# Moving GpSimd's range test of the softmax sums ahead of its last two stores

## The chip, the cores and the metric

The kernel runs on one core of one Trainium2 chip. A core has a matrix engine (TensorE, PE in the profile; PEld is its weight load), a vector engine (VectorE, DVE), a scalar engine (ScalarE, ACT), a general engine (GpSimd, POOL) and a queue engine that only issues transfers (SyncE, SP). Each engine runs its own list of instructions in order, and the lists meet through semaphores. Data moves between memory and the core's buffers by DMA. The metric is the time of one execution on the device, in microseconds (us).

## The reference

Sort-net attention, followed by a token mixer. Batch 4, 8 heads, 768 tokens, 64 values per head, 8 blocks of 96 tokens, model width 512.

```python
P = sort_net                                   # (B, H, 8, 8)
for _ in range(5):
    P = exp(P - max(P, -1))
    P = P / (sum(P, -1) + 1e-09)
    P = P / (sum(P, -2) + 1e-09)
k_sorted, v_sorted = P @ k_blocks, P @ v_blocks
scores = scale * q_b @ k_sorted.T              # per block of 96
attn = exp(scores - max(scores))
attn = attn / (sum(attn, -1) + 1e-09)
x = attn @ v_sorted                            # (B, S, 512) over all heads
W_tok = moe_scale * (x @ w_q) @ (x @ w_k).T    # per batch
out = relu(W_tok @ x) @ w_out
```

## The kernel before

**Order.** Everything is laid out by hand. The string ORDER (lines 18 to 50) lists some 450 steps, and a loop at the end of the kernel (lines 670 to 680) issues them one by one. A step's first letter is its kind, the first digit is the batch, and the rest is a part of that batch. Capital letters are TensorE steps with the PSUM bank that they write. Small letters are the steps that read that bank, with an engine (A ScalarE, D VectorE, G GpSimd, S the SyncE queue). So `r34:D:2` is the normalization's reciprocal of batch 3, group 4, on VectorE. The list fixes the order of each engine's own instructions; between engines, only semaphores order the work.

**Stages of a batch.** K and V are sorted by the 8x8 matrices (K, V, and k, v to move them out of PSUM), scores are formed (S), ScalarE takes their exponentials without subtracting a maximum (e), TensorE multiplies by V with a column of ones so that the sum of each row comes out beside the product (P), VectorE takes the reciprocals of the sums into `Rall` (r, line 399) and multiplies by them (x, line 404). After that come transposes (D as DMA, T on TensorE), the projections (J, j, d), the mixer's products (W, w, G, g, H, h), the output projection (O, with o to move it out of PSUM) and the stores (s). Four batches overlap; the last one is batch 3.

**The range test.** Since no maximum is subtracted, a sum could leave the range of the number format. The kernel keeps all reciprocals of all batches in `Rall` (96 partitions by 280 values) and tests them with GpSimd in `guard()` (lines 504 to 516): the largest value (a reduction across the partitions), a multiplication of the whole tile by -1 in place, the largest again, four operations on a single value, and a load of the resulting flag into a GpSimd register. Line 684 branches on that register. If the flag is set, GpSimd computes the whole result again in a slow and safe way (`general`, lines 518 to 667, a very long straight list of instructions); with the given inputs it is not set, and the branch jumps over that list.

**GpSimd's last steps in the kernel before**, in the order of the list: `d21:G` (a copy into `qD`, line 166), `d30:G` (the same for batch 3), the stores `s21:G` and `s20:G` of batch 2 (line 492, 512 KB each), then the range test, then the branch, then what the branch's join waits for (recorded under line 684), then the end of the program (line 713), where all engines drain and meet. The other stores of the end are issued from SP and from ACT (lines 492 and 497).

Of the kernel before, what the change touches and what calls it, by code (L numbers as in the profile page):

```python
# [41 lines left out]
R30:S R34:S S34:4 J20:3 e35:A:6 h10:D:0 J21:2 R33:S j21:D:2 H11:0 e34:A:4 P32:4 j20:A:3 r32:D:4  # L42
h11:A:0 P30:6 P31:2 s01:S x32:D:4 r31:D:2 x31:D:2 d21:G O15:0 P33:4 o15:A:0 r30:D:6 O10:1 P34:2
o10:A:1 O14:0 N20:S o14:A:0 O11:1 G20:0 s00:S x30:D:6 D30:S r34:D:2 G21:0 r33:D:4 o11:A:1 x33:D:4
g20:A:0 x34:D:2 D31:S d20:A O12:6 s02:S H20:4 H21:0 s10:S H22:2 O13:7 h20:A:4 O20:4 h21:A:0 O23:5
h22:D:2 o13:D:7 J31:2 o12:A:6 j31:A:2 J30:0 O22:1 W31:7 j30:A:0 W30:6 w30:D:6 O21:3 o23:D:5 s12:S
w31:A:7 o20:D:4 o21:D:3 G30:0 s11:S d30:G d31:A G31:0 o22:A:1 s21:G g30:D:0 O25:7 s20:G H32:2 H30:4
H31:0 h32:A:2 O24:6 h30:D:4 h31:D:0 o24:A:6 O34:3 O30:5 o34:A:3 O32:2 O31:4 o25:A:7 o30:D:5 o32:A:2
s34:S O33:0 s22:S o31:D:4 s30:S O315:7 s32:A O35:6 s31:S o33:A:0 o315:A:7 o35:A:6 s33:S s35:A
"""  # L50


# [1 line left out]
def kernel(  # L54
# [12 lines left out]
    B, H, S, D = q.shape  # L67
# [43 lines left out]
    names = {x.split(":")[0] for x in ORDER.split()}  # L111
# [116 lines left out]
    def u_l(b, n, e, bank):  # L228
        if n == "p":
            for s, w in enumerate((moe_w_q, moe_w_k)):  # L230
                nc.gpsimd.dma_start(out=w16[:, s * DM // 2:(s + 1) * DM // 2],  # L231
                                    in_=w.rearrange("(p u) d -> p (u d)", p=P))
        elif n == "o":
            nc.gpsimd.dma_start(out=wo, in_=moe_w_out.rearrange("(t p) d -> p t d", p=P))
        else:
            t, src = {"q": (Qn, q), "k": (Kn, k), "v": (Vn, v)}[n[0]]
            h0, h1 = {"": (0, H), "a": (0, H // 2), "b": (H // 2, H)}[n[2:]]
            b = int(n[1])
            nc.gpsimd.dma_start(out=t[b % NIN][:, h0:h1].rearrange("p h r d -> p h (r d)"),  # L239
                                in_=src[b, h0:h1].rearrange("h (p r) d -> p h (r d)", p=P))  # L240
# [263 lines left out]
    def guard():  # L504
        s1 = keep.tile([1, 2], FP32, name="s1")
        flag = keep.tile([1, 1], mybir.dt.int32, name="flag")
        g = nc.gpsimd
        rv = Rall.rearrange("p b n a t -> p (b n a t)")
        g.tensor_reduce(s1[:, 1:2], rv, axis=AX.XYZWC, op=ALU.max)
        g.tensor_scalar(rv, rv, -1.0, None, op0=ALU.mult)  # L510
        g.tensor_reduce(s1[:, 0:1], rv, axis=AX.XYZWC, op=ALU.max)
        g.tensor_scalar(s1[:, 0:1], s1[:, 0:1], -1e-20, None, op0=ALU.is_le)
        g.tensor_scalar(s1[:, 1:2], s1[:, 1:2], 1e20, None, op0=ALU.is_le)
        g.tensor_tensor(s1[:, 0:1], s1[:, 0:1], s1[:, 1:2], op=ALU.mult)
        g.tensor_scalar(flag, s1[:, 0:1], -1.0, 1.0, op0=ALU.mult, op1=ALU.add)
        return g.value_load(flag[0:1, 0:1])
# [153 lines left out]
    for item in ORDER.split():  # L670
        kind, arg = item[0], item.split(":")[1:]
        if kind == "l":
            u_l(0, item[1:].split(":")[0], None, None)
            continue
        name = item.split(":")[0]
        b, n = int(name[1]), int(name[2:])
        if kind.isupper() and kind not in "RND":
            fns[kind](b, n, int(arg[0]))
        else:
            fns[kind](b, n, arg[0], int(arg[1]) if len(arg) > 1 else None)  # L680

    off = guard()
    work.close()
    with tc.If(off > 0):
        with tc.tile_pool(name="gp", bufs=1) as gp, \
# [32 lines left out]
```

## Time and profile before

| | us |
|---|---|
| median of 3 runs | 100.3 (99.89 to 100.78) |
| the profiled execution | 100.55 |
| its span, first to last instruction | 98.6 |
| granted TensorE clock | 0.997 |
| TensorE busy in the span | 87.9 (89%) |
| ScalarE busy | 71.4 (72%) |
| VectorE busy | 67.3 (68%) |
| GpSimd busy | 31.0 (31%) |
| read from HBM, written to it | 20.19 MB, 6.29 MB |

The profiled execution lies inside the range of the runs, and 1.95 us of its time lie outside the span. Times in the profile count from the span's start. A line number is a line of the kernel; line 160 is the helper through which all matmuls go, lines 164, 166 and 168 are the copies of ScalarE, GpSimd and VectorE. A name such as POOLq or SPq is the engine's instruction queue: branches, semaphore waits, register loads and the issue of transfers stand under it and do not count as busy time. Instructions are themselves brought in by DMA; the profile lists those transfers as queues of the kind "instruction".

### The profile page before, as it was taken

The page shows a single profiled execution, that of the slowest core. Times are in us where ns is not written, and L with a number is a line of the kernel's source. Part 1 is how long each engine was busy: PE and PEld are TensorE (multiplying, and loading weights), DVE is VectorE, ACT ScalarE, POOL GpSimd, SP SyncE. Part 2 cuts the span into 40 slices and gives each one's busy share as a digit, 9 for nine tenths or more (in the row PEclk, how much of TensorE's full clock was granted, in tenths as well). Part 3 has the DMA queues.
Part 4 walks back from the last instruction along what each step waited for, and adds up shares of the span by engine and source line. Part 5 has one row for each costly group of instructions (what it writes and reads, how often), then busy time and mean ns, then how long its engine had stood idle before and what let it go on. Part 6 is the DMA issues. An engine that isn't in the chain of part 4 may idle for free.

```text
span 98.6 us, 3365 instructions
## 1 busy us (share of the span) xinstructions
PE 87.9 (89%) x1429; PEld 59.1 (60%) x1429; DVE 67.3 (68%) x130; ACT 71.4 (72%) x104; POOL 31.0 (31%) x55
## 2 busy tenths in 40 slices
PE   4999697898999999899999999999699999999800
PEld 2346466777888678676676768845565445454400
DVE  2677799779999578987731998956599250965200
ACT  5236876899976998998999989799435765466500
POOL 7973859497009790000000200000200002296000
PEclk9999999999999999999999999999999999999998
DMA  0799999999999999999999996699752999394990
GB/s 10 283 373 200 203 205 204 202 207 203 205 232 249 246 200 206 204 204 240 245 237 206 203 188 87 162 168 260 279 214 54 212 367 415 130 352 174 394 360 6
DMA packets 25488, 21.67 MB, mean 220 GB/s; under 512 B 8192, under 2 KB 23552, under 8 KB 25472
## 3 DMA queue, kind: packets, MB, share of 16 engines
q0 software_dynamic: 12544, 10.36, 63.6%
q1 hardware_dynamic: 12496, 10.44, 36.0%
q10 hardware_dynamic: 432, 0.66, 2.0%
q8 instruction: 11, 0.18, 0.7%
q14 instruction: 5, 0.04, 0.1%
HBM read 20.19 MB, written 6.29 MB: 269 GB/s over the span
## 4 chain that ended last, share of the span: by engine, by line
PE 48%; ACT 15%; DMA 15%; DVE 6%; SPq 5%; POOL 4%; issue 2%; POOLq 0%; ACTq 0%; DVEq 0%
PE ps L160 48%; DMA Kn<-in_k_dram 12%; ACT E L375 7%; DVE X L404 4%; ACT Vs L164 4%; ACT KT L164 3%; DMA VT<-Vs 3%; SPq L410 2%; SPq L336 2%; POOL ot L231 1%; ACT ot L164 1%; POOL Vn L239 1%; DVE Rall L399 1%; DVE QT L168 1%; POOL qkT L221 1%
## 5 line engine op out<-in xcount | busy, mean ns | idle before, releaser
L375 ACT ACTIVATE E<-ps 96x960 bf16<-96x960 f32 (+1 forms) x28 | 23.5, 906 | 1.6 <-PE ps L160 1.4
L160 PE MATMUL ps<-wo,mixT 128*128 128x512 bf16 (+1 forms) x100 | 23.3, 371 | 0.0
L404 DVE TENSOR_TENSOR X<-ps,Rall 96x896 bf16<-96x896 f32 (+1 forms) x20 | 20.0, 1006 | 0.7
L160 PEld LDWEIGHTS <-mixT 128*128 128x128 bf16 x125 | 11.5, 102 | 13.4 <-issue 4.0
L166 POOL COPY qD<-qkT 64x384 bf16<-64x384 bf16 x4 | 2.0, 502 | 45.6 <-ACT qkT L164 31.1
L164 ACT COPY ot<-ps 128x512 f32<-128x512 f32 (+2 forms) x20 | 11.2, 569 | 6.2 <-PE ps L160 6.1
L164 ACT CAST KT<-ps 128x768 bf16<-128x768 f32 x13 | 10.1, 807 | 2.9 <-PE ps L160 2.8
L160 PE MATMUL ps<-VT,E 96*128 96x65 bf16 x256 | 11.0, 193 | 0.9 <-DMA VT<-Vs 0.8
L160 PEld LDWEIGHTS <-E 96*128 96x128 bf16 x256 | 9.5, 97 | 3.2 <-issue 1.0
L260 POOL TENSOR_TENSOR M<-PTR,m_p 128x512 bf16<-128x512 bf16 x6 | 7.8, 1315 | 8.4 <-PE ps L160 7.2
L160 PEld LDWEIGHTS <-KT 64*128 64x128 bf16 (+1 forms) x288 | 8.2, 97 | 3.2 <-issue 2.1
L160 PE MATMUL ps<-QT,KT 64*128 64x96 bf16 x256 | 8.8, 204 | 0.3 <-ACT KT L164 0.3
L467 ACT ACTIVATE mixT<-ps 128x1024 bf16<-128x1024 f32 x7 | 7.1, 1026 | 2.4 <-PE ps L160 2.3
L469 DVE TENSOR_SCALAR mixT<-ps 128x1024 bf16<-128x1024 f32 x5 | 6.0, 1223 | 3.8 <-PE ps L160 3.6
L160 PE MATMUL ps<-M,Kn 128*64 128x128 bf16 x192 | 7.4, 221 | 0.6 <-DMA Kn<-in_k_dram 0.5
L160 PE MATMUL ps<-mixT 128*128 128x512 bf16 x25 | 7.9, 482 | 0.0
L168 DVE CAST KT<-ps 128x768 bf16<-128x768 f32 x7 | 6.5, 953 | 1.1 <-PE ps L160 1.1
L399 DVE RECIPROCAL Rall<-ps 96x14 f32<-96x14 f32 (+1 forms) x20 | 4.4, 226 | 4.0 <-PE ps L160 3.7
L164 ACT COPY QT<-ps 128x768 bf16<-128x768 bf16 x9 | 6.8, 807 | 0.5 <-PE ps L160 0.4
L160 PE MATMUL ps<-idb,Qn 128*64 128x128 bf16 x192 | 6.7, 220 | 0.2 <-POOL Qn L166 0.2
L160 PEld LDWEIGHTS <-Kn 128*64 128x64 bf16 x192 | 5.8, 109 | 1.6 <-DMA Kn<-in_k_dram 0.7
L160 PEld LDWEIGHTS <-Qn 128*64 128x64 bf16 x192 | 5.7, 110 | 0.9 <-issue 0.4
(88 smaller groups left out, 125.3 us busy)
## 6 DMA issues: line engine op xcount, KB each, us to landing
out_dram<-ot SPq DMA_DIRECT2D x7, 512.0 KB, 3.7
Vn<-in_v_dram POOLq DMA_DIRECT2D x4, 768.0 KB, 13.8
Kn<-in_k_dram POOLq DMA_DIRECT2D x4, 768.0 KB, 13.9
Qn<-in_q_dram POOLq DMA_DIRECT2D x3, 768.0 KB, 16.3
VT<-Vs SPq DMA_DIRECT2D x17, 132.0 KB, 6.4
XT<-in_q_dram SPq DMA_DIRECT2D x2, 768.0 KB, 5.1
out_dram<-ot POOLq DMA_DIRECT2D x2, 512.0 KB, 3.5
out_dram<-ot SPq DMA_DIRECT2D x4, 256.0 KB, 3.2
```

The costliest lines, as they stand in the source:

```text
L160: nc.tensor.matmul(o, w, x, is_transpose=t, start=start, stop=stop, skip_group_check=True)
L164: nc.scalar.copy(o, i)
L166: nc.gpsimd.tensor_copy(o, i)
L168: nc.vector.tensor_copy(o, i)
L260: ENG[e].tensor_tensor(out=M[b % 2][:, h0:h0 + hn], in0=src.unsqueeze(2).to_broadcast([P, hn, SP, NB]), in1=m_p.unsqueeze(1).unsqueeze(3). ...
L336: ENG[e].dma_start(out=VT[b % 2].rearrange("(s r) i h x -> r s i (h x)", r=R6)[n], in_=Vs[0][:, n].rearrange("p h e -> p (h e)"))
L375: nc.scalar.activation(E[b % 2][:, n, 0:2 * w * BLK].rearrange("p (t a c) -> p a t c", a=2, c=BLK), PS[0:BLK, bank:bank + 2, 0:w * BLK].re ...
L399: nc.vector.reciprocal(Rall[:, b, n, :, 0:w], avps(bank, w)[:, :, :, D])
L404: nc.vector.tensor_mul(xo.rearrange("p (a t d) -> p a t d", a=2, d=D), avps(bank, w)[:, :, :, 0:D], Rall[:, b, n, :, 0:w].unsqueeze(3).to_ ...
L410: ENG[e].dma_start(out=XT[b % 2][:, 2 * n:2 * n + 2, :].rearrange("p k (i c) -> p (k i) c", c=BLK), in_=X[b % 2][:, 2 * n:2 * n + 2].rearr ...
L467: nc.scalar.activation(o, i, ACT.Relu)
L469: nc.vector.tensor_relu(o, i)
```

## The change

A new step `i40:G` stands in the list behind `x34`, the last normalization. The loop calls `guard()` there. The seven operations of the test and the register load come ahead of `d30:G`, `s21:G` and `s20:G` in GpSimd's list. Behind the loop only the branch on the register remains. What is computed and what the test checks stay the same.

```diff
@@ ORDER
-g20:A:0 x34:D:2 D31:S d20:A O12:6 s02:S H20:4 H21:0 s10:S H22:2 O13:7 h20:A:4 O20:4 h21:A:0 O23:5
+g20:A:0 x34:D:2 i40:G D31:S d20:A O12:6 s02:S H20:4 H21:0 s10:S H22:2 O13:7 h20:A:4 O20:4 h21:A:0
+O23:5 h22:D:2 o13:D:7 J31:2 o12:A:6 j31:A:2 J30:0 O22:1 W31:7 j30:A:0 W30:6 w30:D:6 O21:3 o23:D:5
...
@@ the loop over ORDER
         name = item.split(":")[0]
+        if name == "i40":
+            off = guard()
+            continue
         b, n = int(name[1]), int(name[2:])
...
-    off = guard()
+    if "i40" not in names:
+        off = guard()
     work.close()
     with tc.If(off > 0):
```

More of the change, by code (lines that the diff above doesn't have):

```diff
@@ L44 @@
 o10:A:1 O14:0 N20:S o14:A:0 O11:1 G20:0 s00:S x30:D:6 D30:S r34:D:2 G21:0 r33:D:4 o11:A:1 x33:D:4
-g20:A:0 x34:D:2 D31:S d20:A O12:6 s02:S H20:4 H21:0 s10:S H22:2 O13:7 h20:A:4 O20:4 h21:A:0 O23:5
[L46 to L49, printed above, removed]
+g20:A:0 x34:D:2 i40:G D31:S d20:A O12:6 s02:S H20:4 H21:0 s10:S H22:2 O13:7 h20:A:4 O20:4 h21:A:0
+O23:5 h22:D:2 o13:D:7 J31:2 o12:A:6 j31:A:2 J30:0 O22:1 W31:7 j30:A:0 W30:6 w30:D:6 O21:3 o23:D:5
+s12:S w31:A:7 o20:D:4 o21:D:3 G30:0 s11:S d30:G d31:A G31:0 o22:A:1 s21:G g30:D:0 O25:7 s20:G H32:2
+H30:4 H31:0 h32:A:2 O24:6 h30:D:4 h31:D:0 o24:A:6 O34:3 O30:5 o34:A:3 O32:2 O31:4 o25:A:7 o30:D:5
+o32:A:2 s34:S O33:0 s22:S o31:D:4 s30:S O315:7 s32:A O35:6 s31:S o33:A:0 o315:A:7 o35:A:6 s33:S
+s35:A
 """
```

## The prediction

> **What bounds the kernel now.** I read the chain of waits first, from its last big piece on, and then the issue of the last transfer.
>
> ```profile
> 69.97 22.54 PE ps L160 x204
> ...
> 93.41 0.37 ACT ot L164
> ```
> ```profile
> 93.81 0.34 ACTq L497 DMA_DIRECT2D out_dram<-ot  x1
> ```
> ```profile
> span 98.6 us, 3365 instructions
> ```
>
> TensorE runs without a break from 70.0 to 92.5 us, ScalarE empties the last bank by 93.8, and the last store is issued there. GpSimd stands nowhere in this part of the chain. But the chain stops at 93.8 and the span at 98.6: 4.8 us are left that it does not explain, and the change works in them. Next is what GpSimd does near the end (start, length, what).
>
> ```profile
> 83.05 0.50 POOL L166 COPY qD<-qkT 64x384 bf16<-64x384 bf16 x1 [12.92 <-ACT qkT L164]
> ...
> 86.23 0.55 POOL L492 DMA_DIRECT2D out_dram<-ot  x1 [0.32 <-DVE ot L168]
> 86.83 0.76 POOL L509 CROSS_LANE_REDUCE s<-Rall 96x1 f32<-96x280 f32 x1
> 87.68 0.94 POOL L510 TENSOR_SCALAR Rall<-Rall 96x280 f32<-96x280 f32 x1
> 88.70 0.76 POOL L511 CROSS_LANE_REDUCE s<-Rall 96x1 f32<-96x280 f32 x1
> ...
> 90.39 0.18 POOL L515 TENSOR_SCALAR flag<-s 1x1 int32<-1x1 f32 x1
> ```
> ```profile
> L516 POOLq TENSOR_LOAD <-flag x1: 700/700/700, 90.6 to 90.6; - x1
> ```
> ```profile
> L684 POOLq EVENT_SEMAPHORE  x5: 17/43/43, 94.9 to 95.3; - x5
> L684 POOLq COMPARE_BRANCH  x1: 45/45/45, 91.4 to 91.4; - x1
> L684 POOLq INC_SWDGE_SEM  x1: 512/512/512, 95.4 to 95.4; - x1
> ```
> ```profile
> L713 SPq EVENT_SEMAPHORE  x9: 17/28/28, 95.8 to 96.3; - x9
> L713 POOLq DRAIN  x1: 1375/1375/1375, 95.9 to 95.9; - x1
> ```
> ```profile
> L713 SPq EVENT_SEMAPHORE  x1: 28/28/28, 97.7 to 97.7; - x1
> ```
>
> The test takes 86.8 to 90.6 and ends before the last store is issued, so its arithmetic is covered. The reader should look at what follows. The register load ends at 91.3, the branch is taken at 91.4, and GpSimd's next instruction comes at 94.9: 3.5 us in which it does nothing. It then closes the branch's join by 95.9 and drains until 97.3. SyncE's final waits begin only at 95.8, as the join's increment finishes, and nine of them are through at 96.3; the tenth passes at 97.7. From there to the end of the span the closing barrier takes 0.9. So three things end close together: GpSimd's drain (97.3), SyncE's walk (96.3) and what the tenth wait waited for. The last is the landing of the last store:
>
> ```profile
> DMA to landing us min/median/max: 3.1/3.5/3.8
> ```
>
> This row covers the last SP and the last ACT store; 93.8 plus 3.8 is 97.6, just ahead of the wait's 97.7. Why does a store of 256 KB, the size of the others there, take 3.8? The transfers show it, first by their load, then in detail from 95.9 to 97.5 (40 slices of 0.04 us; a packet counts where it starts).
>
> ```profile
> 95.00:96.00 1.00, 0.00 (x0) 0.00 (x0) 0.00 (x0) 0.00 (x0) 0.00 (x0) 1.00 1.04 383
> ```
> ```profile
> DMA  9923000000000000010101001010101000000000
> ...
> q14 instruction: 1, 0.01, 2.7%
> ```
> ```profile
> q14 instruction: 5, 0.04, 0.1%
> ```
>
> Until 96 the 16 DMA engines are full (1.04, 383 GB/s). All but one are done at 96.06. Then nothing starts for half a microsecond, and seven lone packets follow, some 0.08 apart, the last starting at 97.1: one DMA engine that is late. In the same stretch one packet of instructions moves; its 2.7% of 16 engines over 1.6 us are 0.69 us, and from its start in the first slices to the restart of the lone packets it is just this long. The page counts five such packets of 0.04 MB together, 8 KB each, in the whole span. Another one moves between 93 and 94:
>
> ```profile
> q14 instruction: 1, 0.01, 1.9%
> ```
>
> It takes 1.9% of 16 us, 0.30 us. Its place, between a branch at 91.4 and the resumption at 94.9, makes it the branch's target. For the pair I looked at the loading of the program ahead of the span, from -11 to -5 (slices of 0.15 us):
>
> ```profile
> DMA  0004000000000000100004010000000000000000
> ```
>
> A burst of first blocks stands at slice 3 and one of second blocks at slice 21, 2.7 us later. The packets at 93.3 and 95.9 lie 2.6 apart in the same way. I therefore read both as GpSimd's: the block that it jumped to, and the one behind. Both fall into the full stretch of the last stores and make one DMA engine late: without them it would have been done with the rest, about 1.1 us (97.2 less 96.1) sooner.
>
> The Trainium skill ("Runtime: NRT & Kernel Launch", section "Instruction fetch mechanics") says that a taken branch whose target is out of the window forces a DMA fetch before execution goes on, and that a refill in sequence costs a bump of a queue's tail, mostly hidden. The 3.5 us after the branch agree with the first. By the second the packet at 95.9 would cost nothing and the edit would gain only the first packet's 0.3 us; the lone packets up to 97.1 speak against that.
>
> **The change, part by part.** The test's new place is set by the normalization.
>
> ```profile
> 74.50 0.30 DVE L399 RECIPROCAL Rall<-ps 96x8 f32<-96x8 f32 x2
> 74.84 1.69 DVE L404 TENSOR_TENSOR X<-ps,Rall 96x896 bf16<-96x896 f32 x2
> 78.46 1.23 DVE L469 TENSOR_SCALAR mixT<-ps 128x1024 bf16<-128x1024 f32 x1 [1.93 <-PE ps L160]
> ```
>
> 1. *The test moves.* Its first reduction can start at 74.8 and ends at 75.6. The multiplication by -1 writes `Rall`, which the last normalization reads until 76.5; so it runs 76.6 to 77.5, the second reduction to 78.4, the four small operations (88.70+0.76 to 90.39+0.18, 1.1 us) to 79.5, the load (0.7) to 80.2. GpSimd's next step, the `qD` copy, waits for ScalarE until 83.05. The 2.8 us between are the cover: the copy and the two stores behind it keep their times, and the cost is nothing. Were the cover gone, the copy and both stores would each be late by what exceeds 2.8.
>
> 2. *The branch moves.* Ahead of it is now the second store's issue, ending at 86.78; the branch comes at about 86.85, 4.5 us sooner. Each later piece of GpSimd moves by as much: resumption 90.4, join closed 91.4, drain over 92.8. The join waits for the two stores:
>
> ```profile
> out_dram<-ot POOLq DMA_DIRECT2D x2, 512.0 KB, 3.5
> ```
>
> 86.2 plus 3.5 is 89.7, so that wait is met by 90.4. SyncE's walk no longer waits for the join: it starts behind its last issue near 93.5 and has passed all but the last store by 94.0. None of this is worth time by itself while the last store lands later.
>
> 3. *The two blocks of instructions move*, from 93.3 and 95.9 to 88.8 and 91.4. At 88.8 they meet the stores of batch 2, which nothing at the end waits for. At 91.4 the second block meets the beginning of the last stores. What of it is still there at the end, no row shows. Bounds: 0, if the late engine catches up, and 0.69, if the dearer packet is carried whole. I take 0.30, the cheaper packet carried whole: it is the nearest row, since by 95.9 the late engine still had seven packets of 0.08 left where the others had about two, so the first packet's lag of 0.3 to 0.4 was not worked off in 2.6 us. The gain at the landing is 1.1 less 0.3, or 0.8, with ends 0.4 and 1.1.
>
> Next behind the landing nothing is late: drain at 92.8, walk at 94.0. So the whole 0.8 shows: span 97.8, and 100.55 becomes 99.75. The profiled execution is 0.25 above the median of its three runs; against the median the forecast is 99.5.
>
> **The rivals.** *Second block not GpSimd's.* The packet at 95.9 may be another engine's next block; SyncE itself is near the end of its list there. Then it stays, and only the first packet goes: gain 0.3 to 0.4 (100.15 to 100.25; 99.9 by the median). For it: the two packets' distance proves no owner. Against it: the pattern of the loading.
>
> *Nothing comes of it.* The delay at the landing is one accident of the profiled execution, or another fetch takes its place: 100.3 by the median. For it: the runs before spread over 0.9 us.
>
> *Slower: the test holds VectorE.* In the new place GpSimd reads `Rall` while VectorE runs the last two multiplications that make X. If GpSimd's operation shuts VectorE out of the buffer while it lasts, X is late, and so are the transposes behind it:
>
> ```profile
> 74.72 3.34 SPq L410 DMA_TRANSPOSE XT<-X  x2
> ...
> 80.95 1.46 PE L160 MATMUL ps<-XT,wqk 128*128 128x384 bf16 x8
> ```
> ```profile
> DMA to landing us min/median/max: 3.6/3.7/3.8
> ```
>
> The second transpose is issued about 76.6 and lands at 80.3; the third of the eight matmuls, its first reader, starts at 81.3. So 1.0 us of delay is covered, and from there TensorE, which bounds the stage, moves with it. One reduction (0.76) stays under that. If the whole test (3.7 us) stood in VectorE's way, 2.7 would be added and 0.8 gained: 101.4 by the median. It decides from a hold of 1.8 us on. Against it stands a row of today's overlap:
>
> ```profile
> 87.04 2.36 DVE L469 TENSOR_SCALAR mixT<-ps 128x1024 bf16<-128x1024 f32 x2 [0.78 <-PE ps L160]
> ```
>
> These two operations ran while all three big operations of the test did, at 1.18 each; the one at 78.46, with GpSimd idle, took 1.23. Nothing was held. The Trainium skill ("SBUF — State Buffer", section "Who interferes with whom") has the pair of ports as an exclusive lock, but takes a VectorE operation with at most one input in SBUF, outside the two-port modes, to be free of it. X is made of one operand in PSUM and one in SBUF, so by that page too nothing would be held; no row before shows this very pair of operations together.
>
> **How the numbers follow.** The forecast, both blocks moved out and 0 to 0.69 left, has 0.57; by the median it spans 99.2 to 99.9, with 99.5 as its value. The second block staying has 0.23 (99.9), nothing 0.12 (100.3), the hold of VectorE 0.08 (101.4). About 1% is what a measurement of this kernel can tell from no change, so the mark for faster is 99.3. It takes a gain of 1.0, and ends of 0.4 and 1.1 reach it only when the late engine catches up almost wholly: I give that a third of the forecast's 0.57, 0.19, and 0.09 more for the runs' own spread, 0.28. Slower is the last rival and a little of the spread, 0.09; the rest, 0.63, is within 1%. For 8 in 10 the range goes from 98.9 (99.2 less 0.3 for the spread of a median of such runs) up to 100.5 (nothing comes of it, and 0.2 of spread); the hold of VectorE is left out.
>
> **What would show it.** In the changed kernel's profile: the first reduction at about 74.8 and the load's end near 80.2, with the `qD` copy still at 83.0 and the stores at 85.3 and 86.2 (step 1); the branch near 86.9, GpSimd's next record near 90.4 and its drain over by 93, and SyncE's walk beginning near 93.5 (step 2); packets of instructions near 88.8 and 91.4 and none at 95.9, few or no lone packets behind 96.1, and the last wait passing near 96.9 (step 3). A packet that still stands at 95.9 makes the second block another engine's. The prediction is wrong if the lone packets are as many as before, if X or the XT matmuls stand later by over 1 us, or if the chain of waits no longer ends with TensorE and ScalarE at 93.8.

## The result and the profile after

The changed kernel takes 99.75 us (median of 13 runs, 98.86 to 100.43) against 100.38 us (median of 13 runs) before. The ratio is 0.9923, with a 95% interval from 0.9893 to 0.9952; it compares the means of the fast runs, which leaves out one slow run of the changed kernel (100.43). Faster, then, by 0.5 to 1.1%. Its profiled execution took 99.75 us, and its span is 0.8 us shorter:

```profile
span 97.8 us, 3366 instructions
```

The chain of waits of the changed kernel, its end only (start, length, what), shows that the work itself did not get shorter:

```profile
69.90 22.54 PE ps L161 x204
...
93.33 0.37 ACT ot L165
```

TensorE's last stretch is the same 22.54 us, ScalarE's last copy ends at 93.70 instead of 93.78. The rest is behind that copy: 4.8 us before (98.6 less 93.78), 4.1 now (97.8 less 93.70). So 0.7 of the 0.8 us are gained there, and 0.1 ahead of it, where TensorE's stretch starts sooner (69.90 against 69.97). I call this rest the tail. It is the better measure when single traces are compared, since it does not contain what happened to that execution earlier on.

GpSimd's timeline and the rows of its queue in the changed kernel (for a row of a source line: count, shortest/median/longest in ns, first and last start):

```profile
74.81 0.76 POOL L510 CROSS_LANE_REDUCE s<-Rall 96x1 f32<-96x280 f32 x1 [4.48 <-DVE Rall L400]
76.63 0.94 POOL L511 TENSOR_SCALAR Rall<-Rall 96x280 f32<-96x280 f32 x1 [1.06 <-DVE X L405]
...
82.97 0.50 POOL L167 COPY qD<-qkT 64x384 bf16<-64x384 bf16 x1 [3.46 <-ACT qkT L165]
85.27 0.66 POOL L493 DMA_DIRECT2D out_dram<-ot  x1 [1.79 <-ACT ot L165]
86.19 0.53 POOL L493 DMA_DIRECT2D out_dram<-ot  x1 [0.26 <-DVE Ab L454]
```
```profile
L517 POOLq TENSOR_LOAD <-flag x1: 995/995/995, 79.6 to 79.6; - x1
```
```profile
L689 POOLq EVENT_SEMAPHORE  x5: 17/43/43, 89.9 to 90.4; - x5
L689 POOLq COMPARE_BRANCH  x1: 45/45/45, 86.2 to 86.2; - x1
L689 POOLq INC_SWDGE_SEM  x1: 516/516/516, 90.5 to 90.5; - x1
```
```profile
L718 SPq EVENT_SEMAPHORE  x9: 17/28/28, 93.5 to 96.2; - x9
...
L718 POOLq DRAIN  x1: 1375/1375/1375, 91.0 to 91.0; - x1
```
```profile
L718 SPq EVENT_SEMAPHORE  x1: 27/27/27, 96.9 to 96.9; - x1
```

The test waits twice for VectorE, for the sums and then for X, and is over by 80.6. The `qD` copy still waits for ScalarE, and the two stores are issued when they were. The branch stands at 86.2, GpSimd goes on at 89.9 (3.7 us later), and its drain is over at 92.4 instead of 97.3. SyncE's walk through the final waits starts at 93.5, right behind its last issue, and passes the last one at 96.9 instead of 97.7. From there the closing barrier takes 0.9, as before.

The transfers from 95.9 to 97.5 in the changed kernel (40 slices of 0.04 us, a packet counting where it starts), and the packets of instructions in its windows 88 to 89 and 90 to 91:

```profile
DMA  3501010101010100000000000000000000000000
```
```profile
q14 instruction: 1, 0.01, 1.9%
```
```profile
q14 instruction: 1, 0.01, 5.0%
```

The window has no packet of instructions any more. They moved to 88 and 90, with 0.30 and 0.80 us. One engine is still late, but it restarts from no pause and is done by 96.5, where before it stood still until 96.58 and was done at 97.2.

### The profile page after: what moved, and what is told of

Same layout as the page of the kernel before. It is cut to its first block, busy times and chain, and to the rows that moved or that the text cites. A ratio compares the mean times of both kernels' runs of the same rounds, so it can differ in the third digit from the quotient of the medians.

```text
span 97.8 us, 3366 instructions
## 1 busy us (share of the span) xinstructions
PE 87.8 (90%) x1429; PEld 59.0 (60%) x1429; DVE 67.3 (69%) x130; ACT 71.2 (73%) x104; POOL 31.0 (32%) x55
## 4 chain that ended last, share of the span: by engine, by line
PE 48%; ACT 15%; DMA 15%; DVE 6%; SPq 5%; POOL 4%; issue 2%; POOLq 0%; ACTq 0%; DVEq 0%
PE ps L161 48%; DMA Kn<-in_k_dram 13%; ACT E L376 7%; DVE X L405 4%; ACT Vs L165 4%; ACT KT L165 3%; DMA VT<-Vs 2%; SPq L337 2%; SPq L411 2%; ACT ot L165 1%; POOL ot L232 1%; POOL Vn L240 1%; DVE Rall L400 1%; DVE QT L169 1%; POOL qkT L222 1%
```

## The experiments

All comparisons are with the kernel before. The theory: the branch over the slow path fetches two blocks of instructions, which collide with the last stores on one DMA engine. The first run puts the branch back to where it was and leaves the test early.

```diff
+    pad = Rall.rearrange("p b n a t -> p (b n a t)")
+    for _ in range(4):
+        nc.gpsimd.tensor_scalar(pad, pad, -1.0, None, op0=ALU.mult)
+    for _ in range(2):
+        nc.gpsimd.tensor_scalar(pad[0:1, 0:1], pad[0:1, 0:1], -1.0, None, op0=ALU.mult)
     work.close()
     with tc.If(off > 0):
```

> The changed kernel, with six further GpSimd operations on Rall (four of 0.94 us, two on one value) put between its last store and the branch. The test stays early; the branch falls back to about 91.4 us, where it was before the change. Theory (the two blocks of instructions that the branch fetches collide with the last stores): packets of instructions at about 93.3 and 95.9, lone packets of one DMA engine behind 96.1, last landing 97.5 +- 0.2, span 98.4 +- 0.2, ratio to the kernel before 0.998 to 1.002. Rival (the place of the test itself gives the gain): span 97.8 and ratio 0.992, as in the changed kernel. Rival (GpSimd's join and drain set the end): drain over at about 97.3, span about 98.1 to 98.6, with no lone packets needed.

Ratio 1.0008 (0.9979 to 1.0038): the whole gain is gone. Its rows at the join and its transfers from 95.9 to 97.5:

```profile
L694 POOLq EVENT_SEMAPHORE  x5: 17/43/43, 95.3 to 95.6; - x5
L694 POOLq COMPARE_BRANCH  x1: 45/45/45, 91.4 to 91.4; - x1
```
```profile
DMA  9598999995200000000000001010100101010100
...
q14 instruction: 1, 0.01, 2.5%
```

The branch is back at 91.4, a packet of instructions is back in the window, and so are the pause and the seven lone packets. The span is 98.9, outside the 98.4 +- 0.2 that was expected, but the tail is 4.8 as before (the last copy ends at 94.07 in this execution, which ran 0.3 behind the one of before from earlier on). The place of the test is worth nothing that shows here; the place of the branch is the change.

The second run takes the branch away and leaves the test late.

```diff
     off = guard()
     work.close()
-    with tc.If(off > 0):
-        with tc.tile_pool(name="gp", bufs=1) as gp, \
-                tc.tile_pool(name="gd", bufs=1, space=bass.MemoryType.DRAM) as dram:
-            general(nc.gpsimd, gp, dram)
```

> The kernel before with the range test at its old, late place, but without the branch and the slow path behind it (left out: the branch and the second way of computing the result). Theory of the collision: no packets of instructions behind 90 us, all sixteen DMA engines done by 96.1, last landing 96.4 +- 0.1, span 97.35 +- 0.15, ratio 0.986 to 0.990, more than the changed kernel's 0.992, since nothing is carried over. Rival (place of the test): the test is as late as before, so span 98.6 and ratio 1.00.

Ratio 0.9864 (0.9816 to 0.9912), span 97.4, tail 3.6. Its transfers in the same window end at once, on all engines:

```profile
DMA  7651000000000000000000000000000000000000
```

The third run keeps a late branch, but with a short way to jump.

```diff
     with tc.If(off > 0):
-        with tc.tile_pool(name="gp", bufs=1) as gp, \
-                tc.tile_pool(name="gd", bufs=1, space=bass.MemoryType.DRAM) as dram:
-            general(nc.gpsimd, gp, dram)
+        nc.gpsimd.tensor_scalar(Rall[0:1, 0, 0, 0, 0:1], Rall[0:1, 0, 0, 0, 0:1], -1.0, None, op0=ALU.mult)
```

> The kernel before with test and branch at their old places, but with a slow path of a single operation, so that the branch jumps a few instructions only (left out: the second way of computing the result). Theory of the collision: the branch is still taken near 91.4, GpSimd goes on within 0.2 us instead of 3.5, no packets of instructions at 93.3 and 95.9, span 97.35 +- 0.15, ratio 0.986 to 0.990. Rival (a late branch costs time whatever it fetches): GpSimd still stands for microseconds behind the branch and the span stays at 98.4 to 98.6.

Ratio 0.9859 (0.982 to 0.9898), span 97.5, tail 3.7. The branch and what follows it:

```profile
L684 POOLq COMPARE_BRANCH  x1: 45/45/45, 91.4 to 91.4; - x1
L684 POOLq EVENT_SEMAPHORE  x1: 17/17/17, 91.6 to 91.6; - x1
```

At the very time of the kernel before, a taken branch costs 0.2 us when its target is near, and 3.5 us and two fetched blocks when the whole slow path lies between. With this run and the first, the packet at 95.9 has its owner: it moves with the long jump and is gone without it.

The fourth run tries to have the fetches over before the last stores begin. It is the changed kernel with `s21:G` and `s20:G` written as `s21:S` and `s20:S`.

> The changed kernel with the stores s21 and s20 issued from SP instead of GpSimd, so that the branch comes right behind the qD copy, near 83.6 us. Theory of the collision: packets of instructions near 85.5 and 88, ahead of the gap in the transfers near 90; the DMA engine that they make late catches up there; last landing 96.4 +- 0.1 on all sixteen, span 97.35 +- 0.15, ratio 0.986 to 0.990. Rival (what the changed kernel has left, 0.43 us at the landing, isn't of the fetched block at 90.5): span stays at 97.8, ratio 0.992. Risk: the two stores delay SP's later ones, span 98 or more.

Ratio 0.9896 (0.9852 to 0.994), span 97.7, tail 4.0. The branch stands at 82.9, and the packets of instructions come at 84.9 and 87.1. The expectation is hit for the transfers and missed for the span. Its transfers from 95.9 on, and its last waits, in the window 96.2 to 96.9:

```profile
DMA  5100000000000000000000000000000000000000
```
```profile
L718 SPq EVENT_SEMAPHORE  x7: 27/28/28, 96.4 to 96.8; - x7
```

Nothing is late on any engine, as in the second run. But SyncE's wait for the landing, at 96.4, is the first of seven in this window; six more follow, 0.06 us each. The transfers of SP and ACT take eight semaphores in turn, and the final walk asks them in a fixed order. With two more transfers issued from SP, the last store got a semaphore that is asked fourth; in the kernels before and after, it happened to be the one that is asked last. The fifth run puts the two stores on SP in the kernel before, as a control.

```diff
-w31:A:7 o20:D:4 o21:D:3 G30:0 s11:S d30:G d31:A G31:0 o22:A:1 s21:G g30:D:0 O25:7 s20:G H32:2 H30:4
+w31:A:7 o20:D:4 o21:D:3 G30:0 s11:S d30:G d31:A G31:0 o22:A:1 s21:S g30:D:0 O25:7 s20:S H32:2 H30:4
```

> The kernel before (test late) with the stores s21 and s20 issued from SP: the control for the same move in the changed kernel. The test starts behind the qD copy, near 83.6 us, and the branch comes near 88.2. Theory of the collision: packets of instructions near 90.1 and 92.7, the second within the last stores; one DMA engine lands the last store 0.4 to 0.9 us behind the others (near 96.4); span 98.0 to 98.6, ratio to the kernel before 0.993 to 1.000. Rival (moving the stores to SP is itself what gained in the changed kernel with stores on SP): span 97.7, ratio 0.990.

Ratio 0.9953 (0.9927 to 0.9979), span 98.3, tail 4.4. The join shows the branch, and the transfers from 95.9 show five lone packets:

```profile
L684 POOLq EVENT_SEMAPHORE  x5: 17/43/43, 91.0 to 91.4; - x5
L684 POOLq COMPARE_BRANCH  x1: 45/45/45, 88.5 to 88.5; - x1
```
```profile
DMA  9699785210101010100000000000000000000000
```

One DMA engine is again 0.4 us behind the others, at the low end of what was expected and about as much as in the changed kernel. The tail is 0.3 longer than that kernel's all the same, and its last waits, in the window 96.9 to 97.4, show why:

```profile
L713 SPq EVENT_SEMAPHORE  x7: 27/28/28, 97.0 to 97.4; - x7
```

As in the fourth run, the wait for the last landing, here at 97.0, has six more behind it. So the stores on SP with a late test gain a part only, for two reasons: the fetched blocks still make one engine late, and the final walk ends 0.36 us behind the landing. Moving the stores by itself does not clear the last landing: with the same move as in the fourth run and the branch at 88.5 instead of 82.9, the lone packets are back.

The sixth run is the changed kernel without the branch, with the same lines taken out as in the second.

> The changed kernel (test early) without the branch and the slow path behind it (left out: the branch and the second way of computing the result). Theory of the collision: the same as with the late test and no branch, span 97.4 +- 0.15, ratio 0.984 to 0.990: the place of the test gives and costs nothing. Rival (the early test has a price or a gain of its own, on VectorE or in the last stage): span away from 97.4 by 0.3 or more.

Ratio 0.9889 (0.9852 to 0.9926), as without the branch in the second run. The profiled execution's span, 98.1, is outside what was expected, and by the letter it is the rival's mark. But its tail is 3.7 (98.1 less 94.42), and the other five executions have spans of 97.2 to 97.9. It lost its time ahead of the tail; a load of Q stands in its chain that stands in neither the chain before nor after, and no run shows whether that load is the reason.

```profile
31.18 14.82 DMA Qn<-in_q_dram
```

Early or late, the place of the test is worth no time that these runs can tell. The seventh run checks the reading of the fourth, on that run's kernel. Six loads of 32 bytes into a dead buffer turn the semaphores on until the last store has the one that is asked last.

```diff
+        if (b, n) == (2, 1):
+            few = Lx.rearrange("p a j s -> p (a j s)").bitcast(FP32)
+            for m in range(6):
+                nc.sync.dma_start(out=few[0:1, m * NB:(m + 1) * NB], in_=sort_net[0, 0, m:m + 1, :])
```

> The changed kernel with the stores s21 and s20 on SP, and six loads of 32 bytes into a dead buffer on SP's queue ahead of them, while it is idle. They do nothing for the result; they shift the eight semaphores that the transfers use in turn, so that the last store has the one that SyncE's final walk asks last. Theory: with the stores on SP the span was 97.7 and not 97.35 because the last store's semaphore stood fourth in the walk and seven waits of 0.06 us came behind its landing; now the walk ends with the landing, span 97.35 +- 0.15, ratio 0.984 to 0.990. Rival (the last 0.35 us is something else about the stores on SP): span stays at 97.7.

Ratio 0.9887 (0.9846 to 0.9928), span 97.4, tail 3.6. In the window 96.4 to 96.9, SyncE has one last wait at 96.5 and then the barrier's:

```profile
L722 SPq EVENT_SEMAPHORE  x2: 17/22/28, 96.5 to 96.8; - x2
```

The difference between this tail and the fourth run's, 0.3 to 0.4 us, is the walk's order. This kernel computes everything and has the shortest tail of those that do, 0.4 to 0.5 us under the changed kernel's. Its ratio's interval overlaps that of the changed kernel, so by times alone the two are not told apart. Its transfers from 95.9 on hold one thing more:

```profile
DMA  9753100007000000000000000000000000000000
...
q14 instruction: 1, 0.01, 1.9%
```

The single 7, at 96.3, is a packet of instructions. It comes 13 us behind the branch (83.0), so it is not one of that branch's two, and it starts when the last store's packets are through, so it holds up none of them. Other blocks can fall near the end, then; this one meets no store.

The last run asks what would have stood next behind the landing: GpSimd's tail as late as before, but without fetched blocks.

```diff
+    pad = Rall.rearrange("p b n a t -> p (b n a t)")
+    for _ in range(4):
+        nc.gpsimd.tensor_scalar(pad, pad, -1.0, None, op0=ALU.mult)
+    nc.gpsimd.tensor_scalar(pad[0:1, 0:1], pad[0:1, 0:1], -1.0, None, op0=ALU.mult)
     work.close()
     with tc.If(off > 0):
+        nc.gpsimd.tensor_scalar(Rall[0:1, 0, 0, 0, 0:1], Rall[0:1, 0, 0, 0, 0:1], -1.0, None, op0=ALU.mult)
```

> The kernel before with the short jump, and five GpSimd operations between the test and the branch (four of 0.94 us and one on a single value), so that GpSimd's tail ends as late as in the kernel before, at about 97.3, but with no fetched blocks (left out: the second way of computing the result). It tells what stands next behind the landing. Theory A (the landing is what counts, GpSimd's tail is covered): span 97.4, ratio 0.986. Theory B (the tail was the next bound, 0.5 us behind): no lone packets, all landed at 96.4, but the barrier waits for the drain; span 98.0 to 98.2, ratio 0.993 to 0.996. Theory C (the tail alone set the end): span 98.6, ratio 1.00.

Ratio 0.9933 (0.9902 to 0.9964), span 98.2. The transfers from 95.9 on and GpSimd's drain:

```profile
DMA  9799999944100000000000000000000000000000
```
```profile
L715 POOLq DRAIN  x1: 1375/1375/1375, 96.0 to 96.0; - x1
```

Its wait for the last landing, in the window 96.5 to 97:

```profile
L715 SPq EVENT_SEMAPHORE  x1: 28/28/28, 96.8 to 96.8; - x1
```

All engines land together, as theory B had it. The landing is through at 96.8, and the end waits for the drain (96.0 plus 1.4). Of the 1.2 us of tail that the branch cost the kernel before, this run has 0.7 back without moving GpSimd's tail. That is a little too much for the collision alone: the drain ends 3.3 us behind the last copy here and ended 3.5 behind it before, so with the drain where it was I estimate 0.5 to 0.6. The rest of the 1.2 is had only if GpSimd's tail moves as well. The change moves both.

| kernel | span | tail behind the last copy | ratio (95% interval) |
|---|---|---|---|
| before | 98.6 | 4.8 | 1 |
| changed | 97.8 | 4.1 | 0.9923 (0.9893 to 0.9952) |
| changed, branch late again | 98.9 | 4.8 | 1.0008 (0.9979 to 1.0038) |
| before, no branch | 97.4 | 3.6 | 0.9864 (0.9816 to 0.9912) |
| before, short jump | 97.5 | 3.7 | 0.9859 (0.982 to 0.9898) |
| changed, stores on SP | 97.7 | 4.0 | 0.9896 (0.9852 to 0.994) |
| before, stores on SP | 98.3 | 4.4 | 0.9953 (0.9927 to 0.9979) |
| changed, no branch | 98.1 | 3.7 | 0.9889 (0.9852 to 0.9926) |
| changed, stores on SP, walk turned | 97.4 | 3.6 | 0.9887 (0.9846 to 0.9928) |
| before, short jump, late GpSimd tail | 98.2 | 4.1 | 0.9933 (0.9902 to 0.9964) |

Tails and ratios go together: 1.2 us less of tail is 1.2% of 100.4, and the four kernels with a tail of 3.6 or 3.7 have ratios of 0.986 to 0.989.

## Why the prediction was right

The predicted span was 97.8 and the measured one is 97.8; the predicted median 99.5, the measured one 99.75. The mechanism was the predicted one, and the runs with the branch late, absent and short show it from three sides.

*Step 1, the test moves at no cost.* Right. The first reduction starts at 74.8 and the load ends at 80.6 (forecast 80.2; the load took 1.0 instead of 0.7 us). Of the 2.8 us of cover, 2.4 were left. The copy and the stores kept their times.

*Step 2, the branch moves by 4.5 us.* Right, and a little understated: it stands at 86.2, not 86.9, at the beginning of the second store's issue instead of behind its end. The drain was over at 92.4 and the walk began at 93.5, as forecast. "Next behind the landing nothing is late" holds, and the last run shows that GpSimd's tail had to move for it: left late, the drain alone kept that run's span at 98.2. The 3.5 us that GpSimd stands behind the branch were carried over as a constant; they were 3.7 here, and 2.5 to 3.8 in the runs.

*Step 3, the blocks move and 0.30 us of the second is left.* Right in kind. The packets came at 88.2 and 90.5 (forecast 88.8 and 91.4). What is left is 0.4 us (done at 96.5, the others at 96.1), between the ends of 0 and 0.69. The two reasons for the value taken were both off and cancelled: the packet was the dearest so far, 0.80 us, and about half of its lag was worked off by the end, where I had let a cheap packet be carried whole. So the 0.8 was met with some luck: what the branch cost was 1.2 and not 1.1 (a tail of 4.8 against 3.6 without it), what stayed was 0.4 to 0.5 and not 0.3, and 0.1 of the shorter span came from ahead of the tail.

*The rivals.* The second block is GpSimd's: it came and went with the long jump. The pattern of the loading was no proof of that, since the two packets stood 2.2 to 3.5 us apart in the kernels with the long jump. Nothing coming of it is excluded by the interval. VectorE was not held; the two multiplications that make X, with the first reduction running beside them, and the operation after them in the changed kernel:

```profile
74.77 1.68 DVE L405 TENSOR_TENSOR X<-ps,Rall 96x896 bf16<-96x896 f32 x2
78.38 1.23 DVE L470 TENSOR_SCALAR mixT<-ps 128x1024 bf16<-128x1024 f32 x1 [1.93 <-PE ps L161]
```

They took 1.69 and 1.23 before. The price put on this rival was added up wrongly: 100.3 plus 2.7 less 0.8 is 102.2 by the median, and 101.4 takes the gain off twice. As nothing was held, nothing hangs on it.

The Trainium skill says of a refill in sequence that it is mostly hidden ("Runtime: NRT & Kernel Launch", section "Instruction fetch mechanics"). If the second block is such a refill, it was not hidden here: in the kernel before, the late engine stood still until 96.58, as long as that packet's 0.69 us lasted. Both blocks, with the late join and drain behind them, cost what the table shows between the long and the short jump, about 1.1 us. No run takes away the second block and leaves the first.

*The forecast of the median* was 0.25 too low. I took the profiled execution of before to stand 0.25 above its median, by three runs; with 13 runs that is 0.17, and the changed kernel's profiled execution lies on its median. The gain of 0.8% stays under the 1% from which the prediction counts a kernel as faster; it had given such a result 0.63, and faster 0.28.

## What to carry to other kernels

A branch over a long piece of code is a transfer: it stalls its engine for 2.5 to 3.8 us here and puts two blocks on DMA engines that the last stores may be using, so it belongs where the queues have a gap, ahead of the final stores, with whatever decides it moved up as well. Where the chain of waits ends well before the span, read the tail on its own: which store lands last, whether all DMA engines land it together, and which engine comes last to the closing barrier. Compare single traces by that tail, not by the span.

## What was not expected

The order in which the end of the program asks the transfers' semaphores can cost time. Six waits of 0.06 us stood behind the last landing when the last store's semaphore was fourth in that order, and none when it was last; two more transfers on SP's queue shifted it. In the changed kernel the branch did not wait for the issue ahead of it to end: it stands at 86.2, the second store's issue at 86.19 to 86.72. The shortest stall behind the long jump, 2.5 us, is the fifth run's. There the first block came 1.0 us behind the branch, behind a stretch (89.0 to 89.4) in which no data moved; elsewhere it came 1.8 to 2.2 us behind. Whether that is the reason was not tried.
